# Six loads of a weight matrix begun from ScalarE's DMA queue instead of SyncE's

## The chip, the cores and the metric

The kernel runs on one core of a Trainium2 chip. A core has five engines with an instruction stream each: TensorE (PE in the profile; its weight loads are PEld), VectorE (DVE), ScalarE (ACT), GpSimd (POOL) and SyncE (SP). SyncE does no arithmetic here, it only begins DMA transfers. Sixteen DMA engines move the data. SPq and ACTq are the queues of the DMAs that SyncE and ScalarE begin. The metric is the time of one execution on the device in microseconds (us), shorter is better.

## The reference

Attention with a threshold on the scores (4 batches, 8 heads, 576 positions, width 64), and behind it two gated layers on 2304 tokens of width 512 with an inner width of 2048. All inputs and outputs are fp32.

```python
scores = scale * np.matmul(q, k.transpose(0, 1, 3, 2))
thresh = np.max(scores, axis=-1, keepdims=True) - tau
scores = np.where(scores >= thresh, scores, -1000000000.0)
scores = scores - np.max(scores, axis=-1, keepdims=True)
attn = np.exp(scores)
attn = attn / (np.sum(attn, axis=-1, keepdims=True) + 1e-09)
x = np.matmul(attn, v)                    # heads put side by side: 2304 x 512
...
h = x @ w_in                              # moe: w_in is 512 x 2048
g = h * np.tanh(sp)                       # sp = log1p(exp(h))
x = g @ w_out
...
h = x @ w_in                              # moe2
g = h * np.clip(h + 3.0, 0.0, 6.0) / 6.0
return (g @ w_out).astype(np.float32)
```

## The kernel before

Every instruction belongs to a named step, and the order of all steps is written out by hand in one long string, `SEQUENCE` (line 65), whose words are `step@engine`. Each engine works through its own steps in the order of that string, and a step waits on semaphores for the steps that it needs. So a step that is late holds up everything behind it on its engine.

Steps that matter here, with `n` for a pair of heads, `c` for a tile of 128 queries and `j` for one of the two heads:

- `lk`, `lq`, `lv`: loads of keys (line 1641), queries (1644) and values (1619), begun by SP.
- `s` (1707): scores on PE. `pk` (1716): their row maximum on DVE. `ex` (1726): the exponential on ACT. `th` (1721): the threshold on ACT. `mk` (1729): the mask on DVE, which also frees the score bank. `ph` (1734): rounding to fp16 on ACT. `pl` (629): the fp16 remainder on POOL.
- `tr` (1742): a transpose of the rounded tile by DMA, begun by SP, behind `pl`. `pv` (1755): the product with the values on PE, which needs the transposed tile.
- `dt`, `dr`, `dn`, `fl`, `xh`, `xl`: scaling the result, turning it on PE and splitting it into two fp16 parts, which are the input x of the first layer.

The first input weight, `moe_w_in`, comes as raw 64-bit words in eight groups of 1 MB. For a group `g`, `lr0_g` (line 764) begins the load, `zw0_g` (686, DVE) takes the column maxima, `zd`, `zp`, `zt`, `zf` make a scale of them (ACT, PE, DVE), `c0_g_` (805, ACT) scales and rounds the words, `c0_g_0` and `c0_g_1` (812, POOL) and `c0_g_l` (825, DVE) finish the conversion, and `h0_g_` (845, ACT) and `u0_g_j` (629, POOL) split it into two fp16 parts. Groups 2 and 5 go to a buffer of their own (`rawe`), the others share two (`raw`); a buffer is free again after `c0_g_l`. The products of the first layer, `g..` (1117, PE), start when the first weights and the first 256 rows of x are there, and run between the attention steps until the attention is done. `t` (1165) takes their results out on ACT and `hs` (1173) stores them. The other weights follow later in the same way, with `lr1`, `lr2` and `lr3`.

All eight `lr0` loads are begun by SP, so in its stream they stand between transposes and other loads. `load_words` makes these steps:

Of the kernel before, what the change touches and what calls it, by code (L numbers as in the profile page):

```python
# [77 lines left out]
vm2_1@dve lr0_2@sp ex2_1_0@act fl0_0@pe pk2_1_1@dve pv1_0_0@pe vm1_1@dve xh0_0@act th2_1_0@act c0_1_0@pool tr2_0_0@sp  # L78
# [7 lines left out]
ph0_2_0@act dt2_0@dve s0_3_0@pe zw0_3@dve c0_2_1@pool ph0_2_1@act s1_2_0@pe dr2_0@dve pl0_2_0@pool lr0_4@sp dn2_0@dve
pk0_3_0@dve fl2_0@pe pv3_0_0@pe pk0_3_1@dve ex0_3_0@act xh2_0@act th0_3_0@act xl2_0@dve ex0_3_1@act pv3_1_0@pe
c0_2_0@pool mk0_3_0@dve tr0_2_0@sp mk0_3_1@dve ph0_3_0@act s0_4_0@pe c0_2_l@dve ph0_3_1@act s1_2_1@pe zd0_3@act
pl0_3_0@pool zp0_3@pe dt3_0@dve pk0_4_0@dve zt0_3@dve th0_4_0@act lk0_4@sp dr3_0@dve zf0_3@dve ex0_4_0@act lq0_4@sp
pk1_2_0@dve h0_2_@act mk0_4_0@dve tr0_3_0@sp zx0_0_1@act u0_2_0@pool dn3_0@dve ph0_4_0@act pk1_2_1@dve fl3_0@pe  # L90
ex1_2_0@act pv0_2_0@pe zw0_4@dve th1_2_0@act ex1_2_1@act mk1_2_0@dve xh3_0@act c0_3_@act vm3_1@dve s1_3_0@pe lr0_5@sp
zd0_4@act mk1_2_1@dve s1_3_1@pe c0_3_1@pool ph1_2_0@act ph1_2_1@act s1_4_0@pe pk1_3_0@dve pl0_4_0@pool pk1_3_1@dve
ex1_3_0@act xl3_0@dve th1_3_0@act ex1_3_1@act u0_2_1@pool tr0_4_0@sp mk1_3_0@dve zp0_4@pe zt0_4@dve g00_0_0_0@pe
zf0_4@dve c0_3_0@pool g00_2_0_0@pe g00_4_0_0@pe lk0_5@sp g00_6_0_0@pe c0_4_@act lq0_5@sp g00_8_0_0@pe g00_10_0_0@pe
qp4@pool c0_3_l@dve g01_0_0_0@pe g01_2_0_0@pe pv0_3_0@pe c0_4_0@pool h0_3_@act lr0_6@sp g01_4_0_0@pe dt0_2@dve
# [10 lines left out]
ex2_3_0@act pl2_2_0@pool g31_4_0_0@pe g31_6_0_0@pe zf0_5@dve ex2_3_1@act g31_8_0_0@pe hs1_0_0@sp g31_10_0_0@pe
g40_0_0_0@pe th2_3_0@act xs0_4@sp g40_2_0_0@pe vh4@act g40_4_0_0@pe mk2_3_0@dve pv1_3_0@pe zx0_0_2@act mk2_3_1@dve
ph2_3_0@act u0_4_1@pool tr2_2_0@sp g40_6_0_0@pe g40_8_0_0@pe c0_5_@act dt1_2@dve dr1_2@dve zw0_6@dve s2_4_0@pe
s3_2_0@pe t3_0_0@act dn1_2@dve c0_5_0@pool pk2_4_0@dve ph2_3_1@act g40_10_0_0@pe g41_0_0_0@pe lr0_7@sp g41_2_0_0@pe
c0_5_1@pool pk3_2_0@dve g41_4_0_0@pe th2_4_0@act lk0_6@sp g41_6_0_0@pe ex2_4_0@act fl1_2@pe lq0_6@sp pv1_4_0@pe  # L110
# [474 lines left out]
def fused_kernel(ctx: ExitStack, tc, q, k, v, tau, w1i, w1o, w2i, w2o, out):  # L585
    nc = tc.nc
# [3 lines left out]
    add = plan.add  # L590
# [1447 lines left out]
```

## Time and profile before

| | |
|---|---|
| median of 3 runs | 966.33 us (966.15 to 967.31) |
| the profiled execution | 967.36 us, of which 965.5 us are the span from the first to the last instruction |
| PE busy | 920.3 us, 95% of the span |
| DVE, ACT, POOL busy | 767.3, 647.9, 402.5 us |
| DMA issues by SP | 217 plain ones and 80 transposes |

The profile comes from a single execution. Its views give, among others, the busy time of each engine by stretches of the span; a timeline of instructions by engine, with the idle time before each and what ended it in square brackets; the chain of work that ended last; and for DMA issues the time to landing. A row of a timeline has the start, the duration, engine, line, operation, output and inputs, and how many instructions are merged in it. For SPq and ACTq the duration is that of the issue on the queue, not that of the transfer. PEclk is the share of its full clock that TensorE was granted.

### The profile page before, as it was taken

What the parts mean: (1) busy time and instruction counts of PE and PEld (TensorE: products, weight loads), DVE (VectorE), ACT (ScalarE), POOL (GpSimd) and SP (SyncE); (2) the same over time, 40 slices, a digit from 0 to 9 for tenths busy, and PEclk for the clock granted to TensorE, in tenths of its full rate; (3) what the DMA queues carried; (4) which work ended last, traced back from release to release, by engine and by line L of the source; (5) the groups of instructions that cost most, each with busy time, mean ns of one, the idle gap of its engine ahead of it and who ended that gap; (6) DMA issues with size and microseconds to landing.
All of it is one profiled execution on the core that took longest, in us unless ns stands there. A gap on an engine that the chain in (4) does not pass through costs nothing.

```text
span 965.5 us, 25780 instructions
## 1 busy us (share of the span) xinstructions
PE 920.3 (95%) x10776; PEld 796.3 (82%) x10776; DVE 767.3 (79%) x1432; ACT 647.9 (67%) x1051; POOL 402.5 (42%) x354
## 2 busy tenths in 40 slices
PE   4679799999999999999999999999999999999998
PEld 2457577777777788888888888999999999999997
DVE  7997888778879887469999879787758858847865
ACT  6779877888789876568866878565444545536541
POOL 2778775756655766125656777710000000000000
PEclk9979999999999999999999999999999999999999
DMA  9999999999999999764665757760110101201001
GB/s 311 225 246 233 262 242 232 256 206 232 224 255 270 210 224 224 253 242 161 235 228 195 273 180 269 248 231 2 61 47 17 61 25 39 62 23 40 24 1 45
DMA packets 201796, 164.46 MB, mean 170 GB/s; under 512 B 174160, under 2 KB 174928, under 8 KB 195280
## 3 DMA queue, kind: packets, MB, share of 16 engines
q1 hardware_dynamic: 201296, 162.62, 62.5%
q8 instruction: 85, 1.39, 0.6%
q10 hardware_dynamic: 384, 0.20, 0.1%
q14 instruction: 31, 0.25, 0.1%
HBM read 84.28 MB, written 36.04 MB: 125 GB/s over the span
## 4 chain that ended last, share of the span: by engine, by line
PE 75%; DVE 15%; DMA 5%; ACT 1%; issue 1%; POOL 1%; SPq 1%; DVEq 0%; ACTq 0%; POOLq 0%
PE h_g L1117 14%; PE y_y L1231 13%; PE s_s L1707 7%; PE hp_g1a L1304 5%; PE h_g0a L1304 5%; PE aux_pv L1755 5%; DMA pt_tr<-p_ph 4%; PE hp_g1d L1304 2%; PE h_g0d L1304 2%; DVE e_ex L1729 2%; DVE nm_pk L1716 2%; DVE top L686 1%; PE h_g1b L1304 1%; PE hp_g0b L1304 1%; DVE gs_gh L1211 1%
## 5 line engine op out<-in xcount | busy, mean ns | idle before, releaser
L629 POOL TENSOR_TENSOR p_ph<-e_ex,p_ph 128x128 f16<-128x128 f32 (+3 forms) x160 | 186.9, 1190 | 119.1 <-ACT p_ph L1734 62.7
L1454 PEld LDWEIGHTS <-gs_oh 128*128 128x128 f16 x1512 | 146.9, 98 | 16.5
L1304 PEld LDWEIGHTS <-w__h 128*128 128x128 f16 x2016 | 156.0, 98 | 0.6
L1729 DVE SCALAR_TENSOR_TENSOR e_ex<-s_s,thr_th,e_ex 128x576 f32<-128x576 f32 x136 | 106.2, 812 | 19.8 <-ACT thr_th L1721 14.3
L1716 DVE TENSOR_REDUCE nm_pk<-s_s 128x1 f32<-128x576 f32 x136 | 98.6, 751 | 23.3 <-PE s_s L1707 22.0
L1726 ACT ACTIVATE e_ex<-s_s,nm_pk 128x576 f32<-128x576 f32 x136 | 98.3, 729 | 20.0 <-DVE nm_pk L1716 18.5
L1734 ACT ACTIVATE p_ph<-e_ex 128x576 f16<-128x576 f32 x144 | 94.8, 679 | 8.7 <-DVE e_ex L1729 6.7
L1304 PEld LDWEIGHTS <-w__u 128*128 128x128 f16 x1008 | 98.6, 98 | 0.0
L1755 PEld LDWEIGHTS <-pt_tr 128*128 128x128 f16 x2016 | 79.3, 101 | 19.2 <-DMA pt_tr<-p_ph 11.2
L1755 PE MATMUL aux_pv<-vh,pt_tr 128*128 128x65 f16 (+1 forms) x1296 | 85.2, 202 | 6.8 <-DMA pt_tr<-p_ph 6.7
L629 DVE TENSOR_TENSOR gs_oh<-g_ab,gs_oh 128x896 f16<-128x896 f32 x72 | 74.6, 1085 | 15.2 <-ACT gs_oh L1404 15.2
L1707 PE MATMUL s_s<-kd_lk,qs_qp 64*128 64x288 f32 x416 | 71.1, 455 | 7.4 <-DVE e_ex L1729 6.3
L1404 ACT ACTIVATE gs_oh<-g_ab 128x1792 f16<-128x1792 f32 x36 | 59.6, 1690 | 27.5 <-DVE g_ab L629 24.4
L1755 PE MATMUL aux_pv<-vl_vl,pt_tr 128*128 128x64 f16 x720 | 69.6, 201 | 0.0
L1388 ACT ACTIVATE g_ab<-g_ab,aux,hscales 128x512 f32<-128x512 f32 x72 | 54.1, 805 | 17.1 <-DVE g_ab L1332 17.1
L1707 PEld LDWEIGHTS s_s<-kd_lk,qs_qp 64*128 64x128 f32 x416 | 37.5, 195 | 26.6 <-issue 15.1
L1202 ACT ACTIVATE hp_e<-hl_l 128x512 f32<-128x512 f32 x72 | 42.5, 596 | 21.2 <-DVE gs_gh L1211 20.7
L1165 ACT ACTIVATE he_t<-h_g,hin 128x512 f32<-128x512 f32 x63 | 42.9, 682 | 18.4 <-PE h_g L1117 14.2
L1394 DVE SCALAR_TENSOR_TENSOR g_ab<-g_ab,f 128x512 f32<-128x512 f32 x72 | 51.2, 745 | 5.0 <-ACT g_ab L1388 5.0
L1211 DVE SCALAR_TENSOR_TENSOR gs_gh<-hp_e,fscales,gs_gh 128x512 f16<-128x512 f32 x72 | 52.8, 741 | 1.7 <-ACT gs_gh L1205 1.7
L1205 ACT ACTIVATE gs_gh<-hp_e,fscales 128x512 f16<-128x512 f32 x72 | 47.4, 680 | 9.9 <-PE y_y L1231 9.3
L1322 ACT ACTIVATE s_ka<-h_g0a 128x512 f32<-128x512 f32 x27 | 16.1, 595 | 48.4 <-PE h_g0a L1304 48.2
(662 smaller groups left out, 2555.8 us busy)
## 6 DMA issues: line engine op xcount, KB each, us to landing
hd<-he_t SPq DMA_DIRECT2D x36, 512.0 KB, 4.2
hl_l<-hd SPq DMA_DIRECT2D x18, 1024.0 KB, 5.6
raw_lr<-in_moe_w_out SPq DMA_DIRECT2D x16, 1024.0 KB, 7.4
raw_lr<-in_moe_w_in SPq DMA_DIRECT2D x14, 1024.0 KB, 6.1
yd<-yl_zhy SPq DMA_DIRECT2D x9, 896.0 KB, 3.6
qs_qp<-in_q SPq DMA_DIRECT2D x11, 576.0 KB, 4.9
v_lv<-in_v SPq DMA_DIRECT2D x16, 320.0 KB, 4.3
kd_lk<-in_k SPq DMA_DIRECT2D x15, 288.0 KB, 4.9
```

Source lines behind the costliest of these rows:

```text
L629: engine[e].tensor_tensor(dst, a, b, ALU.subtract)
L1117: mm(hv[:, j, :], wj[:, wl, c * P : (c + 1) * P], x.tile[:, c, xl, :], start=j == 0 and n == 0, stop=j == 1 and n == 11, skip_group_check= ...
L1211: nc.vector.scalar_tensor_tensor(s.tile[:, k, 1], g.tile.rearrange("p (a n) -> p a n", a=2), fs[:, fp : fp + 1], s.tile[:, k, 0], ALU.mult ...
L1231: mm(yv[:, h, :], wt[1][f // 2].tile[:, f % 2, wl, c * P : (c + 1) * P], gs[fp // COL].tile[:, fp % COL, gl, f % 2, :], start=fp == 0 and ...
L1304: mm(dst.tile[:, i * Q : (i + 1) * Q], wt[2][fp][wl].tile[:, right - 1, c * P : (c + 1) * P], x[xl].tile[:, c, left - 1], start=first and ...
L1454: mm(region(p), part[:, gl, left - 1], wt[3][fp][wl].tile[:, right - 1], start=fp == n == 0 and spot(p)[1] == 0, stop=fp == NG - 1 and n == 2,
L1707: mm(s[j].tile[:, half, :HALF], lh[r], rh[r], start=m == 0, stop=m == len(terms) - 1,)
L1716: nc.vector.tensor_reduce(neg.tile[:, j : j + 1], sv(j), AX.XY, ALU.max, negate=True)
L1726: nc.scalar.activation(ev(j), sv(j), AF.Exp, bias=neg.tile[:, j : j + 1])
L1729: nc.vector.scalar_tensor_tensor(ev(j), sv(j), thr.tile[:, j : j + 1], ev(j), ALU.is_ge, ALU.mult)
L1734: nc.scalar.activation(p16.tile[:, j, :S], e_.tile[:, j], AF.Copy)
L1755: mm(ov[:, dst, :d], pt.tile[:, j, ch, :], part.tile[:, src, vc, :], start=i == j == ch == 0 and part is vh, stop=j == w - 1 and ch == 8, ...
```

## The change

Six of the eight loads of the first input weight, `lr0_2` to `lr0_7`, are begun by ACT. `lr0_0` and `lr0_1` stay with SP, as do the loads of the other three weights, all transposes and all loads of queries, keys and values. The words keep their places in `SEQUENCE` (the rest of the string's diff is re-wrapped lines), so on ACT each load now stands behind the last ACT step that is written ahead of it: `lr0_2` behind `c0_1_`, `lr0_3` behind `ph3_0_1`, `lr0_4` behind `ph0_2_1`, `lr0_5` behind `c0_3_`, `lr0_6` behind `h0_3_` and `lr0_7` behind `ph2_3_1`. The transfers themselves, their buffers and what waits for them are the same.

```diff
-vm2_1@dve lr0_2@sp ex2_1_0@act fl0_0@pe pk2_1_1@dve pv1_0_0@pe vm1_1@dve xh0_0@act th2_1_0@act c0_1_0@pool tr2_0_0@sp
+vm2_1@dve lr0_2@act ex2_1_0@act fl0_0@pe pk2_1_1@dve pv1_0_0@pe vm1_1@dve xh0_0@act th2_1_0@act c0_1_0@pool tr2_0_0@sp
...
+zw0_2@dve fl1_0@pe s3_1_1@pe pl3_0_0@pool lr0_3@act pk3_1_0@dve pv2_0_0@pe pk3_1_1@dve ex3_1_0@act s0_2_0@pe
...
+s0_3_1@pe ph0_2_0@act dt2_0@dve s0_3_0@pe zw0_3@dve c0_2_1@pool ph0_2_1@act s1_2_0@pe dr2_0@dve pl0_2_0@pool lr0_4@act
...
+lr0_5@act zd0_4@act mk1_2_1@dve s1_3_1@pe c0_3_1@pool ph1_2_0@act ph1_2_1@act s1_4_0@pe pk1_3_0@dve pl0_4_0@pool
...
+g00_10_0_0@pe qp4@pool c0_3_l@dve g01_0_0_0@pe g01_2_0_0@pe pv0_3_0@pe c0_4_0@pool h0_3_@act lr0_6@act g01_4_0_0@pe
...
+s2_4_0@pe s3_2_0@pe t3_0_0@act dn1_2@dve c0_5_0@pool pk2_4_0@dve ph2_3_1@act g40_10_0_0@pe g41_0_0_0@pe lr0_7@act
...
     def load_words(raw, src, tag):
         def go(e):
-            nc.sync.dma_start(out=raw.tile, in_=src)
-
-        return add(("sp",), go, [], [raw], tag)
+            queue = nc.scalar if e == "act" else nc.sync
+            queue.dma_start(out=raw.tile, in_=src)
+
+        return add(("sp", "act"), go, [], [raw], tag)
```

## Rows read from the trace of the kernel before

**Rows 1.** The page: busy tenths and clock in 40 slices.
```profile
PE   4679799999999999999999999999999999999998
DVE  7997888778879887469999879787758858847865
```

**Rows 2.** Windows: start and end, length, busy of PE, PEld, DVE, ACT, POOL, PEclk.
```profile
30.00:66.00 36.00, 24.01 (x287) 17.27 (x286) 34.48 (x67) 27.06 (x50) 27.84 (x25) 0.85 1.07 237
66.00:140.00 74.00, 65.98 (x707) 49.24 (x708) 61.82 (x126) 62.46 (x115) 58.48 (x57) 0.91 1.09 248
```

**Rows 3.** Timeline of SP's queue from 34 us.
```profile
34.10 0.59 SPq L1644 DMA_DIRECT2D qs_qp<-in_q  x1
34.74 0.59 SPq L764 DMA_DIRECT2D rawe_lr<-in_moe_w_in  x1
35.51 6.87 SPq L1742 DMA_TRANSPOSE pt_tr<-p_ph  x1
```

**Rows 4.** The same queue from 90 us.
```profile
90.21 3.48 SPq L1742 DMA_TRANSPOSE pt_tr<-p_ph  x1
...
95.10 0.95 SPq L1644 DMA_DIRECT2D qs_lq<-in_q  x1
96.56 6.08 SPq L1742 DMA_TRANSPOSE pt_tr<-p_ph  x1
```

**Rows 5.** DMA issues begun near 34.8, 94.2, 95.1 and 51.5 us; us to landing last.
```profile
rawe_lr<-in_moe_w_in SPq DMA_DIRECT2D x1, 1024.0 KB, 7.5
raw_lr<-in_moe_w_in SPq DMA_DIRECT2D x1, 1024.0 KB, 5.1
qs_lq<-in_q SPq DMA_DIRECT2D x1, 576.0 KB, 7.5
v_lv<-in_v SPq DMA_DIRECT2D x1, 320.0 KB, 3.3
```

**Rows 6.** The chain that ended last: start, us, what.
```profile
34.10 4.41 DMA qs_qp<-in_q
...
96.56 9.04 DMA pt_tr<-p_ph
```

**Rows 7.** Timeline of PE, two of its waits.
```profile
38.56 0.76 PE L1707 MATMUL s_s<-kd_lk,qs_qp 64*128 64x288 f32 x4 [0.70 <-DMA qs_qp<-in_q]
...
105.65 0.20 PE L1755 MATMUL aux_pv<-vh,pt_tr 128*128 128x65 f16 x1 [1.25 <-DMA pt_tr<-p_ph]
```

**Rows 8.** Timeline of DVE around 40 us and at 74 us.
```profile
39.36 0.76 DVE L1716 TENSOR_REDUCE nm_pk<-s_s 128x1 f32<-128x576 f32 x1
40.33 0.76 DVE L1716 TENSOR_REDUCE nm_pk<-s_s 128x1 f32<-128x576 f32 x1 [0.21 <-PE s_s L1707]
...
74.42 0.16 DVE L1792 TENSOR_SCALAR den_dt<-aux_pv 128x4 f32<-128x4 f32 x1 [1.37 <-PE aux_pv L1755]
```

**Rows 9.** Timeline of ACT: what follows the places of three moved loads.
```profile
33.87 0.73 ACT L1726 ACTIVATE e_ex<-s_s,nm_pk 128x576 f32<-128x576 f32 x1
...
37.46 0.68 ACT L1734 ACTIVATE p_ph<-e_ex 128x576 f16<-128x576 f32 x1 [1.25 <-DVE e_ex L1729]
...
45.21 0.74 ACT L1726 ACTIVATE e_ex<-early_s,nm_pk 128x576 f32<-128x576 f32 x1 [1.50 <-DVE nm_pk L1716]
...
93.27 0.29 ACT L1721 ACTIVATE thr_th<-nm_pk,ntau 128x1 f32<-128x1 f32 x1 [0.18 <-DVE nm_pk L1716]
```

**Rows 10.** The two stretches in which ACT begins DMAs: first and last microseconds.
```profile
0.74 0.41 ACTq L600 DMA_DIRECT2D tau_sb<-in_tau  x1
...
961.11 1.86 ACTq L1511 DMA_DIRECT2D out<-s_vg  x3
```

**Rows 11.** Windows as in rows 2, around a fall of the clock.
```profile
96.00:100.00 4.00, 1.39 (x9) 0.64 (x8) 3.93 (x9) 3.12 (x5) 2.67 (x4) 0.96 0.98 339
100.00:104.00 4.00, 4.00 (x44) 2.78 (x41) 2.68 (x7) 3.84 (x8) 3.64 (x5) 0.61 1.16 256
```

More of the change, by code (lines that the diff above doesn't have):

```diff
@@ L86 @@
[L86 to L95, printed above, removed]
@@ L106 @@
[L106 to L110, printed above, removed]
@@ new lines @@
+ex1_4_0@act g10_6_0_0@pe g10_8_0_0@pe pv0_4_0@pe u0_3_0@pool kh0_4@act tr1_2_0@sp mk1_4_0@dve ex2_2_0@act
+g10_10_0_0@pe dt0_4@dve s2_2_1@pe zw0_5@dve u0_3_1@pool ph1_3_1@act xh0_2@act g11_0_0_0@pe ph1_4_0@act g11_2_0_0@pe
+dr0_4@dve c0_4_1@pool xl0_2@dve g11_4_0_0@pe g11_6_0_0@pe pk2_2_1@dve dn0_4@act g11_8_0_0@pe g11_10_0_0@pe ph1_3_0@act
+g20_0_0_0@pe c0_4_l@dve fl0_4@pe g20_2_0_0@pe th2_2_0@act g20_4_0_0@pe t1_0_0@act pl1_3_0@pool g20_6_0_0@pe
+g20_8_0_0@pe mk2_2_0@dve g20_10_0_0@pe ex2_2_1@act g21_0_0_0@pe g21_2_0_0@pe g21_4_0_0@pe xh0_4@act kh0_5@act
@@ new lines @@
+tr3_2_0@sp g51_0_0_0@pe pk4_0_0@dve g51_2_0_0@pe th3_4_0@act g51_4_0_0@pe ex3_4_0@act g51_6_0_0@pe qp7@pool
+u0_6_1@pool dn2_2@dve g51_8_0_0@pe ph3_3_1@act g51_10_0_0@pe zp0_7@pe g60_0_0_0@pe zt0_7@dve fl2_2@pe mk3_4_0@dve
+g60_2_0_0@pe pl3_3_0@pool xh2_2@act g60_4_0_0@pe pv2_4_0@pe t5_0_0@act xl2_2@dve zf0_7@dve ph3_4_0@act lk0_7@sp
+s4_0_1@pe dt2_4@dve c0_7_@act pk4_0_1@dve g60_6_0_0@pe g60_8_0_0@pe pl3_4_0@pool tr3_3_0@sp g60_10_0_0@pe ex4_0_0@act
+dr2_4@dve dn2_4@dve g61_0_0_0@pe g61_2_0_0@pe g61_4_0_0@pe th4_0_0@act g61_6_0_0@pe ex4_0_1@act mk4_0_0@dve
@@ new lines @@
+ph5_1_0@act s6_0_1@pe lv1_2@sp vl6@dve ph5_1_1@act pv4_1_0@pe vh7@act pk6_0_0@dve pl5_1_0@pool g00_6_0_1@pe
+ex6_0_0@act dt4_0@dve g00_8_0_1@pe pk6_0_1@dve g00_10_0_1@pe g01_0_0_1@pe g01_2_0_1@pe dr4_0@dve th6_0_0@act
+g01_4_0_1@pe ex6_0_1@act g01_6_0_1@pe mk6_0_0@dve g01_8_0_1@pe g01_10_0_1@pe tr5_1_0@sp g10_0_0_1@pe mk6_0_1@dve
+t0_0_1@act g10_2_0_1@pe g10_4_0_1@pe g10_6_0_1@pe ph6_0_0@act dn4_0@dve g10_8_0_1@pe g10_10_0_1@pe vm0_2@dve
+g11_0_0_1@pe ph6_0_1@act g11_2_0_1@pe s6_1_0@pe pl6_0_0@pool s6_1_1@pe lv2_2@sp pk6_1_0@dve hs7_0_0@sp fl4_0@pe
@@ new lines @@
+pk6_1_1@dve pv5_0_0@pe ex6_1_0@act zf1_1@dve th6_1_0@act g11_4_0_1@pe ex6_1_1@act g11_6_0_1@pe mk6_1_0@dve
+g11_8_0_1@pe tr6_0_0@sp g11_10_0_1@pe xh4_0@act g20_0_0_1@pe mk6_1_1@dve ph6_1_0@act g20_2_0_1@pe g20_4_0_1@pe
+g20_6_0_1@pe xl4_0@dve ph6_1_1@act s7_0_0@pe vl7@dve s7_0_1@pe t1_0_1@act pl6_1_0@pool pk7_0_0@dve c1_1_@act
+hs1_0_1@sp pv5_1_0@pe pk7_0_1@dve g20_8_0_1@pe ex7_0_0@act dt5_0@dve g20_10_0_1@pe dr5_0@dve vm2_2@dve g21_0_0_1@pe
+g21_2_0_1@pe th7_0_0@act g21_4_0_1@pe ex7_0_1@act mk7_0_0@dve g21_6_0_1@pe c1_1_0@pool g21_8_0_1@pe tr6_1_0@sp
@@ new lines @@
+hs3_0_1@sp th4_2_0@act ex4_2_1@act g40_4_0_1@pe mk4_2_0@dve g40_6_0_1@pe g40_8_0_1@pe g40_10_0_1@pe mk4_2_1@dve
+ph4_2_0@act g41_0_0_1@pe tr7_1_0@sp g41_2_0_1@pe s4_3_0@pe vm3_2@dve ph4_2_1@act s4_3_1@pe dt6_0@dve ve2@dve
+pl4_2_0@pool dr6_0@dve pk4_3_0@dve zdv2_2@act g41_4_0_1@pe g41_6_0_1@pe g41_8_0_1@pe dn6_0@dve g41_10_0_1@pe
+ex4_3_0@act g50_0_0_1@pe pk4_3_1@dve fl6_0@pe pv7_0_0@pe xh6_0@act th4_3_0@act xl6_0@dve ex4_3_1@act g50_2_0_1@pe
+tr4_2_0@sp mk4_3_0@dve g50_4_0_1@pe t4_0_1@act g50_6_0_1@pe g50_8_0_1@pe mk4_3_1@dve g50_10_0_1@pe ph4_3_0@act
@@ new lines @@
+g51_0_0_1@pe s4_4_0@pe ph4_3_1@act s5_2_0@pe pl4_3_0@pool pk4_4_0@dve lk0_8@sp pv7_1_0@pe lq0_8@sp pk5_2_0@dve
+th4_4_0@act ex4_4_0@act g51_2_0_1@pe dt7_0@dve g51_4_0_1@pe dr7_0@dve g51_6_0_1@pe ex5_2_0@act mk4_4_0@dve
+g51_8_0_1@pe g51_10_0_1@pe g60_0_0_1@pe qp8@pool tr4_3_0@sp t5_0_1@act g60_2_0_1@pe dn7_0@dve g60_4_0_1@pe c1_0_l@dve
+g60_6_0_1@pe ph4_4_0@act g60_8_0_1@pe s5_2_1@pe pl4_4_0@pool pk5_2_1@dve fl7_0@pe pv4_2_0@pe xh7_0@act kh0_8@act
+xl7_0@dve tr4_4_0@sp g60_10_0_1@pe g61_0_0_1@pe th5_2_0@act g61_2_0_1@pe ex5_2_1@act mk5_2_0@dve g61_4_0_1@pe
@@ new lines @@
+g61_6_0_1@pe h1_0_@act g61_8_0_1@pe hs5_0_1@sp g61_10_0_1@pe mk5_2_1@dve g70_0_0_1@pe lr1_2@sp s5_3_0@pe ph5_2_0@act
+xs3_4@sp s5_3_1@pe u1_0_0@pool t6_0_1@act pk5_3_0@dve g70_2_0_1@pe ph5_2_1@act pk5_3_1@dve g70_4_0_1@pe pv4_3_0@pe
+ex5_3_0@act pl5_2_0@pool g70_6_0_1@pe th5_3_0@act ex5_3_1@act dt4_2@dve g70_8_0_1@pe dr4_2@dve mk5_3_0@dve
+g70_10_0_1@pe g71_0_0_1@pe g71_2_0_1@pe mk5_3_1@dve g71_4_0_1@pe ph5_3_0@act g71_6_0_1@pe g71_8_0_1@pe g71_10_0_1@pe
+dn4_2@dve ph5_3_1@act s5_4_0@pe tr5_2_0@sp c1_1_l@dve t7_0_1@act s6_2_0@pe pl5_3_0@pool pk5_4_0@dve fl4_2@pe
```

141 lines of the change are left out of this document (58 added, 83 removed).

## The prediction

> **What bounds the kernel now.** I read the page first. In the 40 slices, of 24 us each, PE is at 9 tenths from the sixth slice on, and the early slices are those in which PE has 4 to 7 tenths and DVE up to 9 [rows 1]. So behind some 140 us the time is PE's work, and what this change can win or lose lies ahead of that, where the six loads are begun (34 to 94 us). The windows cut that stretch in two [rows 2]. From 30 to 66 us DVE is busy for 34.48 of 36 us: DVE is the bound, and the most that could be won there, if it never waited, is 36 - 34.48 = 1.5 us. From 66 to 140 us PE has 65.98 of 74 us, and its waits are what can be won.
>
> I then asked whether the loads themselves are late for anyone, in the list of waits from 26 to 100 us: no wait of DVE or ACT for a raw weight word stands in it. So an earlier load is worth nothing by itself. What is left is what the loads do to their neighbours: to SP's stream, to the transfers beside them, and now to ACT's stream.
>
> **SP's side: what is removed.** The load of 34.74 costs SP 0.59 us of issue [rows 3]; six of them are at most 3.5 us. SP is free of it at 35.33 and begins the next transpose at 35.51; behind each of the six there is such a gap, mostly because the transpose waits for POOL's remainder. So the issue time itself gives nothing: POOL sets the pace, and if it didn't, the 3.5 us would be spread over SP's stream, for which DVE doesn't wait.
>
> The transposes behind the loads do gain. The one at 35.51 lasts 6.87 us, to 42.38, and the load of 34.74 lands 7.5 us after its issue, at 42.2 [rows 3, 5]. The one at 96.56 lasts 6.08 us, to 102.64, with the queries of 95.10 landing at 102.6 [rows 4, 5]. Nothing of that kind ahead, a transpose takes 3.48 us (90.21). I read from this that a transpose is held on SP's queue until the plain load ahead of it in the same queue has landed. With the load on ACT's queue this hold goes or shrinks: up to 6.87 - 3.48 = 3.4 us at 35.51, and at 96.56, where 1 MB leaves the queue ahead of keys and queries, up to 6.08 - 3.48 = 2.6 us.
>
> Who waits for these transposes? Ahead of 66 us nobody on the chain, DVE being the bound. At 105.65 PE does: 1.25 us idle for the transpose of 96.56, which took 9.04 us and is on the chain [rows 6, 7]. The landing 1.25 us sooner is well within the 2.6 us, so this wait goes. What comes behind it is not all free, since the next scores need a bank that DVE's mask frees a moment later; bounds 0 and 1.25 us, and I take 1.0 us as the gain, nearer to the full row because other banks are free.
>
> **ACT's side: what is added.** ACT gets six issues. The trace has ACT beginning DMAs only in its first and last microseconds: 0.41 us for one, 1.86 us for three, so 0.41 to 0.62 us each [rows 10], at most 6 x 0.62 = 3.7 us together. Where ACT has slack they are hidden. Behind `ph3_0_1` ACT idles for 1.50 us until 45.21 [rows 9]; `lr0_3` falls there, and `lr0_4` and `lr0_6` fall in two more idle stretches of this sort. `lr0_2` pushes the exponential of 33.87 back by some 0.5 us, and ACT idles for 1.25 us at 37.46 for DVE. `lr0_5` delays `zd0_4` and what follows, near 67 us, and DVE has 1.37 us of waiting at 74.42 [rows 8] that takes it up. `lr0_7` stands in front of the threshold of 93.27, where ACT waited only 0.18 us, and the exponential behind it leads over DVE to PE's scores: 0.41 - 0.18 = 0.2 us lost. No buffer makes ACT wait: that of `lr0_2` is new, and for the other five ACT has, earlier in its own order, done the `h0` step of the group that had the buffer (`h0_3_` stands right ahead of `lr0_6`), and this step waits for the same conversion that frees it.
>
> Whether ACT is held when SP's queue is in the middle of a transpose isn't to be seen, as ACT begins nothing beside one. Bounds: nothing, or until that transpose's issue is over. For `lr0_7`, reached at 93.07, that is until 93.69 and then 0.41 to 0.62 us, so up to 1.0 us instead of 0.2. I take 0.2, the row of a plain issue under traffic, 0.59 us at 34.74, being nearer to it than a hold.
>
> **The transfers: what collides.** Ahead of `lr0_2` SP begins the queries of pair 3 at 34.10; they land 4.41 us later and PE, which has waited for 0.70 us, starts their scores at 38.56 [rows 3, 6, 7]. DVE takes the maxima at 39.36 without any idle time ahead and waits 0.21 us for the second at 40.33 [rows 8]. So these queries are on the path of the engine that is the bound, without slack. In one queue the weight words, begun at 34.74, come behind them. ACT reaches `lr0_2` at about 33.87 [rows 9], so now the 1 MB starts in another queue at about the same moment as the 576 KB. The lower bound of the delay is 0, if SP's queue goes first. The upper bound is the whole of the 1 MB: 1024 KB landed in 5.1 us at best and 320 KB in 3.3 us [rows 5], so 704 KB more cost 1.8 us, and 1024 KB, by estimate from these rows, 2.6 us. With equal shares, 576 KB of the weight words go beside the queries: 576 / 1024 x 2.6 = 1.5 us. I take that. It is paid in full: DVE's order is fixed and it has next to no idle time up to 66 us, and PE's start of the first layer follows it.
>
> The Trainium skill has two rules here, on the page "DMA: Bandwidth & Descriptors". Its section "Queues, rings and completion order" says that SP and ACT each own a row of rings on the same 16 DMA engines, which serve the rows in turn packet by packet, and share the descriptor generator. It speaks for the delay of the queries and for ACT being held; no row of this trace shows two queues at work together, so it can't be tested here. The section "Issuing engines are not separate DMA queues" says that beginning DMAs on several engines saves only the issue time of the sequencer. By that rule the hold behind the loads would not go away and the sum would be that of the third rival below.
>
> **The sum.** On the profiled execution, 967.36 us (965.5 of span and 1.9 around it): +1.5 for the queries, +0.2 for ACT at 93.27, -1.0 for the wait at 105.65, so +0.7 us. The profiled execution is 1.0 us above the median of the runs, 966.33; on the median the sum gives 967.0 us.
>
> **The rivals.** *Slower.* The loads on ACT's queue are served ahead of what SP has begun. Then the whole 1 MB goes ahead of the queries of 34.10 (+2.6 us), and at 94 us `lr0_7`, begun at 93.1 by ACT, still goes ahead of the keys and the queries of 95.10, so that the transpose of 96.56 is held as now and nothing is won at 105.65: 2.6 + 0.2 = +2.8 us, 969.1 us. It decides from the point where two thirds of the 1 MB, (1.9 - 0.2) / 2.6, go ahead of the queries. For it: the load is begun first or together, and the queries have no slack. Against it: nothing in the trace gives ACT's queue the right of way.
>
> *Faster.* The queries land as now, the freed transposes win 1.25 us at 105.65 and 0.2 us of DVE's wait at 40.33, and with the shorter gaps TensorE keeps its clock. Its falls are dear: in the stretch from 96 to 100 us PE is busy for 1.39 of 4 us, and from 100 to 104 us the granted clock is 0.61, so mostly the lower level of 1.2 GHz [rows 11], which costs PE 39% of 4 us, 1.6 us. From 66 to 140 us the clock is 0.91 in the mean [rows 2], so there are more of these. With one fall less the sum is -1.25 - 0.2 - 1.6 = -3.0 us, 963.3 us; if the fall goes in part, 964.0 us. It decides only if a fall goes, since the first two terms are within 1.9 us. Against it: only one of the freed transposes has PE waiting for it. A fall more, as likely with PE's start put off, would go to the slower case.
>
> *Nothing changes.* The hold of the transposes comes from the traffic, not the queue; the loads arrive as before, and ACT's six issues fall into its slack: 966.3 us, within 0.2 us of it.
>
> **How the numbers follow.** No change is what lies within 0.2%, 1.9 us, about what a measurement of this kernel can tell. The sum of +0.7 us has 0.42, of which 0.08 is past +1.9 us; slower has 0.20; faster has 0.24, of which 0.03 stays within 1.9 us; nothing has 0.14. So faster 0.21, same 0.34 + 0.03 + 0.14 = 0.51, slower 0.28. The range leaves out about a tenth on each side: on top that half of the slower case in which a fall of the clock comes on the 2.8 us, so it ends at 970.0; below that part of the faster case in which a whole fall goes, so it begins at 963.8. The likeliest case's own range is 965.5 to 968.9: the delay of the queries at 0 (-1.5 us) or 2.6 us (+1.1), and ACT held on top of that (+0.8).
>
> **What would show it.** The queries at 34.10 should land 5 to 7 us after their issue and DVE should wait over a microsecond at 40.33; if they land in 4.4 us, that step is wrong. The transposes behind the old places of the loads should last 3.3 to 4.5 us on SP's queue; if they still take 5 to 7 us, the reading of the hold is wrong. PE's wait at 105.65 should be gone. ACT's six issues should take 0.4 to 0.6 us; several microseconds would mean that ACT is held. What would make the whole wrong is a fall of the clock that comes or goes, or a load on ACT that waits for something I have not seen and holds up the exponentials.

## The result, and the profile after

The changed kernel takes 978.64 us in the median (976.60 to 980.47, 4 runs), the kernel before 966.82 us beside it (966.15 to 969.41): the ratio is 1.0117, 95% interval 1.0086 to 1.0147. That is slower by 11.8 us, where 967.0 us and no change were forecast, and outside the range of 963.8 to 970.0. The profiled execution has a span of 975.6 us, 10.1 us more than before.

The page of the changed kernel, busy tenths as in [rows 1]:

```profile
PE   4659789999999999999999999999999999999998
DVE  7778689878788888469999889878848847857865
```

And the windows of [rows 2] (the last two numbers are the busy share of the DMA engines and the GB/s that they moved):

```profile
30.00:66.00 36.00, 22.28 (x246) 15.64 (x247) 28.76 (x54) 22.15 (x38) 25.95 (x24) 0.94 0.93 218
66.00:140.00 74.00, 60.49 (x588) 43.72 (x586) 56.75 (x119) 58.11 (x106) 51.55 (x53) 0.85 0.98 223
```

The loss is where it was looked for, ahead of 140 us, but the reader should look at DVE: it is busy for 28.76 of 36 us instead of 34.48, so it is no longer the bound up to 66 us; it waits. PE has 5.5 us less work in the second stretch.

DVE has the same instructions in the same order in both kernels, so its lateness can be read off instruction by instruction. This is the start of some of them against the kernel before, in us, for the two profiled executions (worked out from the timelines):

```
start in the kernel before   36.61  41.45  59.45  61.32  74.42  105.95  110.78  130.02  247.53  960.61
later in the changed one     -0.51   3.37   3.19   7.70   7.08    7.09   11.39   12.31    9.81   10.16
```

The loss comes in three steps: 3.9 us at about 40 us, 4.5 us at 60 us, 4.3 us at 107 us; some 2 us are given back behind 130 us. Each has one of the moved loads beside it. The timeline of the two queues (those of [rows 3] and [rows 4], with ACT's issues of `lr0_2`, `lr0_4` and `lr0_7`):

```profile
30.30 3.39 SPq L1743 DMA_TRANSPOSE pt_tr<-p_ph  x1
...
31.98 0.34 ACTq L765 DMA_DIRECT2D rawe_lr<-in_moe_w_in  x1
...
33.74 0.59 SPq L1645 DMA_DIRECT2D qs_qp<-in_q  x1
34.84 5.55 SPq L1743 DMA_TRANSPOSE pt_tr<-p_ph  x1
...
57.40 0.33 ACTq L765 DMA_DIRECT2D raw_lr<-in_moe_w_in  x1
...
97.29 3.70 SPq L1743 DMA_TRANSPOSE pt_tr<-p_ph  x1
...
97.91 0.34 ACTq L765 DMA_DIRECT2D raw_lr<-in_moe_w_in  x1
...
103.82 8.68 SPq L1743 DMA_TRANSPOSE pt_tr<-p_ph  x1
```

On SP's queue the load stood behind the transpose's issue, 3.4 to 4.0 us after its start. ACT begins it 1.7, 1.2 and 0.6 us after the start (the transpose beside `lr0_4` began at 56.16), while the transpose is still being issued. The DMA issues, with us to landing last, first `lr0_2` and the transpose of 30.30, then the queries of 33.74, then `lr0_4` and the transpose of 56.16, then `lr0_7` and the transpose of 97.29:

```profile
rawe_lr<-in_moe_w_in ACTq DMA_DIRECT2D x1, 1024.0 KB, 6.4
pt_tr<-p_ph SPq DMA_TRANSPOSE x1, 8.2
...
qs_qp<-in_q SPq DMA_DIRECT2D x1, 576.0 KB, 6.6
...
raw_lr<-in_moe_w_in ACTq DMA_DIRECT2D x1, 1024.0 KB, 6.7
pt_tr<-p_ph SPq DMA_TRANSPOSE x1, 7.8
...
raw_lr<-in_moe_w_in ACTq DMA_DIRECT2D x1, 1024.0 KB, 10.6
pt_tr<-p_ph SPq DMA_TRANSPOSE x1, 12.3
```

In the kernel before, the first two of these transposes, of 30.81 and 52.80:

```profile
pt_tr<-p_ph SPq DMA_TRANSPOSE x1, 5.3
...
pt_tr<-p_ph SPq DMA_TRANSPOSE x1, 5.1
```

The third, of 90.21, landed after 5.2 us, the queries after 4.41 us [rows 6] and the load of 94.22 after 5.1 us [rows 5]. So the transposes that were already under way are late by 2.9, 2.7 and 7.1 us, and in the last pair the load is late as well.

In the first two pairs it is only the end of the transpose that is late. A transpose moves 2304 packets of 256 bytes; 32 packets of 4 bytes go with it, and it lands 0.5 to 0.6 us behind the last of these. The packet records of the transpose of 30.30 show the 256-byte packets done at 35.26 (35.62 before), but the 4-byte packets run from 37.39 to 37.83, where they ran from 35.43 to 35.63 before: behind the 128 packets of the load, which run from 35.06 to 37.81. Between 35.4 and 37.0 us 91 packets move, all of them the load's. Beside `lr0_4` it is the same: 256-byte packets done at 60.80, 4-byte packets at 63.38, the load's last at 63.37.

Who pays is in the timeline of PE. Two waits of the kernel before are in [rows 7], 0.70 us for the queries and 1.25 us for the transpose of 96.56; a third was for the transpose of 52.80, here with the scores behind it:

```profile
57.94 0.20 PE L1755 MATMUL aux_pv<-vh,pt_tr 128*128 128x65 f16 x1 [0.67 <-DMA pt_tr<-p_ph]
...
58.96 1.24 PE L1707 MATMUL s_s<-kd_lk,qs_lq 64*128 64x288 f32 x8
```

In the changed kernel:

```profile
38.49 0.23 PE L1756 MATMUL aux_pv<-vh,pt_tr 128*128 128x65 f16 x1 [2.87 <-DMA pt_tr<-p_ph]
...
40.40 1.33 PE L1708 MATMUL s_s<-kd_lk,qs_qp 64*128 64x288 f32 x4 [0.20 <-DMA qs_qp<-in_q]
...
64.06 0.24 PE L1756 MATMUL aux_pv<-vh,pt_tr 128*128 128x65 f16 x1 [3.60 <-DMA pt_tr<-p_ph]
...
65.70 2.29 PE L1708 MATMUL s_s<-kd_lk,qs_lq 64*128 64x288 f32 x8
...
115.43 0.20 PE L1756 MATMUL aux_pv<-vh,pt_tr 128*128 128x65 f16 x1 [4.14 <-DMA pt_tr<-p_ph]
```

and behind PE in that of DVE (39.36 and 40.33 of [rows 8] are here 41.78 and 43.70):

```profile
41.78 0.76 DVE L1717 TENSOR_REDUCE nm_pk<-s_s 128x1 f32<-128x576 f32 x1 [1.38 <-PE s_s L1708]
43.70 0.76 DVE L1717 TENSOR_REDUCE nm_pk<-s_s 128x1 f32<-128x576 f32 x1 [1.16 <-PE s_s L1708]
...
68.04 0.76 DVE L1717 TENSOR_REDUCE nm_pk<-s_s 128x1 f32<-128x576 f32 x1 [2.07 <-PE s_s L1708]
...
118.73 0.76 DVE L1717 TENSOR_REDUCE nm_pk<-s_s 128x1 f32<-128x576 f32 x1 [1.86 <-PE s_s L1708]
```

The waits are not the whole loss: behind each of them PE works at about half its speed for some microseconds. The eight scores of 65.70 take 2.29 us where they took 1.24; the granted clock is 0.50 from 64 to 68 us, the lower level of 1.2 GHz, and was 1.00 from 58.0 to 60.5 in the kernel before. Behind the tile of 115.43 it is 0.57 from 116 to 120 us (1.00 from 106.0 to 108.5 before). At the first step the granted clock reads 1.00, but the scores of 40.40 and the two groups behind them take 1.33, 1.17 and 1.17 us, as they do in `e6_later` at a granted clock of 0.50, and 0.76, 0.65 and 0.65 in the kernel before. PE, too, has the same instructions in the same order in both kernels, and comparing them one by one puts sizes on this (lateness of PE in us, worked out from the timelines):

```
              ahead of the tile   at the tile   behind the scores
first step          -0.5              2.3              3.4
second step          3.2              6.1              7.8
third step           7.0              9.8             11.3
```

At the first step the wait of 0.70 us for the queries has shrunk to 0.20, so that PE is 1.8 us late when the scores begin. So the late tiles cost 2.3, 2.9 and 2.8 us and the slow work 1.5, 1.7 and 1.5 us.

The chain that ended last shows the same transfers: where [rows 6] has queries of 4.41 us and one transpose of 9.04 us, it now has

```profile
33.74 6.62 DMA qs_qp<-in_q
...
56.16 7.85 DMA pt_tr<-p_ph
...
103.82 11.56 DMA pt_tr<-p_ph
```

In the first step it runs over the queries, since they landed 0.16 us behind the moment at which PE was through with the late tile. The transpose of 103.82 is that of [rows 4] at 96.56. Its own load is gone from in front of it, but the transfers ahead of it, and with them its issue (8.68 us instead of 6.08), are late because of the collision at 97.

### The profile page after: what moved, and what is told of

The parts are those of the page before. It is cut to its first block, busy times and chain, and to the rows that moved or that the text cites. A ratio compares the mean times of both kernels' runs of the same rounds, so it can differ in the third digit from the quotient of the medians.

```text
span 975.6 us, 25780 instructions
## 1 busy us (share of the span) xinstructions
PE 925.1 (95%) x10776; PEld 799.2 (82%) x10776; DVE 767.5 (79%) x1432; ACT 648.6 (66%) x1051; POOL 402.5 (41%) x354
## 4 chain that ended last, share of the span: by engine, by line
PE 84%; DVE 9%; DMA 4%; issue 1%; ACT 1%; POOL 0%; SPq 0%; DVEq 0%; ACTq 0%
PE h_g L1118 17%; PE y_y L1232 17%; PE s_s L1708 9%; PE aux_pv L1756 6%; PE h_g0a L1305 5%; PE hp_g1a L1305 5%; DMA pt_tr<-p_ph 3%; PE hp_g1d L1305 2%; PE h_g0d L1305 2%; DVE e_ex L1730 2%; DVE nm_pk L1717 2%; PE h_g1b L1305 1%; PE hp_g0b L1305 1%; PE y_y___1_7_0_14515 L1455 1%; PE y_y___1_6_0_13903 L1455 1%; PE y_y___1_5_0_13243 L1455 1%
## 5 line engine op out<-in xcount | busy, mean ns | idle before, releaser
L1756 PE MATMUL aux_pv<-vh,pt_tr 128*128 128x65 f16 (+1 forms) x1296 | 85.8, 203 | 12.9 <-DMA pt_tr<-p_ph 12.9
L1708 PE MATMUL s_s<-kd_lk,qs_qp 64*128 64x288 f32 x416 | 74.5, 474 | 6.7 <-DVE e_ex L1730 6.3
```

Source lines behind the costliest of these rows:

```text
L1708: mm(s[j].tile[:, half, :HALF], lh[r], rh[r], start=m == 0, stop=m == len(terms) - 1,)
L1756: mm(ov[:, dst, :d], pt.tile[:, j, ch, :], part.tile[:, src, vc, :], start=i == j == ch == 0 and part is vh, stop=j == w - 1 and ch == 8, ...
```

## The experiments

The theory after the result, called collision: a large load begun in a second queue while a transpose of SP's queue is under way makes the transpose, and at times the load too, land late, and the time is lost where PE waits for that transpose at once. The rivals: a cost spread over all six loads (bandwidth, or ACT's issue time), the queries of pair 3 alone (the prediction's own step), and a cost of ACT's queue wherever the load stands. The lateness of DVE in each profile, at the same instructions as above, and the timed ratio to the kernel before:

```
                             36.61  41.45  61.32  74.42  105.95  110.78  130.02  247.53  960.61   ratio, 95% interval
changed kernel               -0.51   3.37   7.70   7.08    7.09   11.39   12.31    9.81   10.16   1.0117 (1.0086 to 1.0147)
e1_lr2                       -0.59   3.36   3.19   2.57    2.59    2.11    2.10    0.41    3.66   1.0012 (0.9999 to 1.0025)
e2_lr457                     -0.23  -0.10   4.81   5.61    5.63    6.84    5.71    3.53    3.94   1.0091 (1.0059 to 1.0123)
e3_lr36                       0.14   0.23   0.71   0.32    0.35   -0.16   -0.16   -3.35   -1.44   1.0000 (0.9983 to 1.0016)
e11_lr7                       0.17   0.24   0.05  -0.09   -0.08    3.70    4.69    2.18    2.36   1.0019 (0.9999 to 1.0040)
e12_quarter                  -0.02   0.03   0.03  -0.13   -0.12   -0.16   -0.09   -1.39   -1.46   1.0014 (0.9997 to 1.0031)
e6_later                     -0.62   1.25   1.06   0.45    0.44    0.10    0.19   -2.86   -2.91   1.0002 (0.9978 to 1.0026)
e9_later_sp2                  0.25   0.42   0.22   0.02    0.02   -0.66   -0.67   -2.47   -1.58   0.9996 (0.9974 to 1.0019)
e5_tiny_dram                  0.17   1.40   1.66   1.07    1.06    1.31    0.07   -1.12   -1.18   0.9999 (0.9981 to 1.0016)
e4_tiny                       0.28   2.17   1.98   1.95    1.98    2.55    2.31    7.71   10.70   1.0084 (1.0062 to 1.0106)
e10_tile                     -0.31   0.01  -0.18  -1.13   -1.12   -1.28   -0.70    0.06    2.75   1.0049 (1.0027 to 1.0071)
```

Up to 130 us the columns are mostly clean steps. Behind 130 us most kernels drift by 1 to 3 us against this one profile of the kernel before, with or without a moved load; the changes are judged by the steps.

**One part at a time.** Three kernels leave some of the six words with SP.

```diff
-lr0_2@sp
+lr0_2@act
```

> Only lr0_2 is begun by ACT, the other five by SP. Theory, collision: a 1 MB load in ACT's queue that starts while a transpose of SP's queue is under way makes both land late, and whoever needs the transpose pays. lr0_2 started beside the transpose of 30.30, which took 8.15 us instead of 5.29; the stretch up to the exponential of before's 45.21 lost 3.3 us. So 969 to 971 us, and the lost time within 30 to 46 us. Rival, spread cost (bandwidth shared, or ACT's issue time): a sixth of the 11.8 us lost in all, 968 to 969 us. Rival, the queries of pair 3 alone (the prediction's step): +1.5 us, with the loss seen at DVE's wait for these scores and the transposes on time.

968.99 us, and the whole loss of 3.9 us sits at 40 us, as in the changed kernel. Some of it is given back by 75 us, and the timed ratio says only 1.2 thousandths, an interval that still holds 1. What PE waited for ahead of the scores of pair 3:

```profile
38.53 0.24 PE L1756 MATMUL aux_pv<-vh,pt_tr 128*128 128x65 f16 x1 [2.99 <-DMA pt_tr<-p_ph]
...
40.38 1.33 PE L1708 MATMUL s_s<-kd_lk,qs_qp 64*128 64x288 f32 x4
```

It waited 2.99 us for the tile of the transpose beside the load, which landed after 8.3 us, and then only 0.14 us, too short for the view to name what ended it: the queries, landed 6.7 us after their issue, were there for scores that were late already. So the rival of the queries alone, which wanted the transposes on time, falls.

```diff
-lr0_4@sp ... lr0_5@sp ... lr0_7@sp
+lr0_4@act ... lr0_5@act ... lr0_7@act
```

> Only lr0_4, lr0_5 and lr0_7 are begun by ACT: the three that started 1.2, 3.4 and 0.6 us behind the start of a transpose that was still under way. Collision: most of what is lost behind 46 us comes back, +6 to +9 us, 973 to 976 us, with each of the three landing 6.5 us or more after its issue and the transpose beside it 8 us or more. Spread cost: half of the loss, +6 us, so about 972.7 us, and then the kernel with lr0_3 and lr0_6 must cost a third, +4 us.

976.07 us: the larger part. `lr0_4`, begun at 54.12, landed after 6.6 us and the transpose of 52.92 beside it after 8.0 us; DVE lost 4.9 us. `lr0_5` and `lr0_7` took 9.3 and 9.9 us and the transposes beside them 12.9 and 10.7 us, but cost DVE only 0.8 and 1.2 us here. Behind the wait at the third step, 3.01 us at 112.49, the granted clock stayed at 1.00 (112.5 to 116.5 us), so the slow work that followed it in the changed kernel is missing. The profile is that of the fastest of the five runs, 971.20 us; it shows less of the loss than the median has.

```diff
-lr0_3@sp ... lr0_6@sp
+lr0_3@act ... lr0_6@act
```

> Only lr0_3 and lr0_6 are begun by ACT: the two that started with no transpose under way (the next one was begun 3.3 and 3.8 us later). Collision: nothing lost, 966 to 968 us. Spread cost (bandwidth, or ACT's issue time, or that the loads leave SP's order): a third of the loss, +4 us, 970.5 us.

966.27 us, nothing lost: the spread cost, which wanted +4 us, falls. But one premise of mine was wrong as well. In this kernel `lr0_3` did start beside a transpose, 0.6 us behind it (42.70 and 43.27); the DMA issues of the two, with us to landing last:

```profile
raw_lr<-in_moe_w_in ACTq DMA_DIRECT2D x1, 1024.0 KB, 6.5
pt_tr<-p_ph SPq DMA_TRANSPOSE x1, 9.7
```

So the collision was there, 9.7 us instead of 6.4. PE waited 1.07 us for that tile at 52.41, but DVE was at most 0.7 us late behind it and on time again by 111 us. The theory has to be in two parts: the collision makes the transpose late, and the place decides who pays.

**One load alone, and a quarter of it.**

```diff
-lr0_7@sp
+lr0_7@act
```

> Only lr0_7 is begun by ACT, at its place in the change, 0.6 us behind the start of a transpose. Theory, collision: the transpose of about 90.2 lands 9 us or more after its begin instead of 5.16, lr0_7 likewise instead of 5.1, and DVE is 3 to 4.5 us late from 108 us on, as it was in the change: 969 to 971 us. Rival, the loss at 108 us came from the lateness brought along from 40 and 60 us: no loss here, 966.8 us, or the gain of 1 us that the prediction gave to the freed transpose behind it.

969.61 us, with 3.8 us lost from 106 to 111 us and none before (the interval of the timed ratio just holds 1). From 74 to 106 us DVE is within 0.1 us of the kernel before, so the same 10 us can be laid side by side. The DMA view of `e11_lr7` from 90 to 100 us, in 40 slices (the tenths are the busy share of the 16 DMA engines; q1 is SP's queue, q10 ACT's; then packets, MB, share), and of the DMA issues begun from 90 to 91 us:

```profile
DMA  9630069996993100192299196099929999999929
GB/s 442 145 79 0 0 128 213 158 40 148 666 36 34 33 0 0 34 201 34 34 237 101 34 237 101 34 372 507 473 105 429 425 291 281 56 118 108 70 8 30
DMA packets 1869, 1.61 MB, mean 161 GB/s; under 512 B 1711, under 2 KB 1711, under 8 KB 1740
...
q10 hardware_dynamic: 144, 1.05, 54.0%
...
raw_lr<-in_moe_w_in ACTq DMA_DIRECT2D x1, 1024.0 KB, 9.5
pt_tr<-p_ph SPq DMA_TRANSPOSE x1, 11.9
```

The same view of the kernel before; then a line of its window from 96 to 98 us, in which only packets of loads move, and the transpose among the issues from 90 to 91 us:

```profile
DMA  9732029993008999999299514898979978989998
GB/s 426 260 77 73 0 53 218 201 44 8 0 5 183 291 287 292 292 290 190 39 131 262 98 33 197 360 524 360 492 262 360 459 295 318 329 313 341 313 258 249
DMA packets 2888, 2.30 MB, mean 230 GB/s; under 512 B 2528, under 2 KB 2528, under 8 KB 2758
...
q1 hardware_dynamic: 92, 0.75, 97.8%
...
pt_tr<-p_ph SPq DMA_TRANSPOSE x1, 5.2
```

Before, from 93 us on (the 13th slice), the transpose moves at 290 GB/s and is done. With the load beside it, the GB/s go to 34 and to 0, with short bursts up to 237, for some 3.5 us, and in the 10 us 1.61 MB move instead of 2.30. So in this pair the two do not only share the rate, the rate falls. A packet of the load takes 10 us x 16 x 0.540 / 144 = 0.60 us in the mean, against 2 us x 16 x 0.978 / 92 = 0.34 us in the kernel before; the 144 include 16 packets of 4 bytes, and the 128 others alone take 0.67 us. That is not so in every pair: the load's packets took 0.32 us beside the transpose of 30.30 and 0.34 us beside that of 56.16, and in the 10 us from the start of the former 2.51 MB moved, against 2.14 MB in the kernel before.

```diff
-g41_0_0_0@pe lr0_7@sp g41_2_0_0@pe
+g41_0_0_0@pe lx0_7@act lr0_7@sp g41_2_0_0@pe
...
-            nc.sync.dma_start(out=raw.tile, in_=src)
+            ps = slice(32, P) if tag == "lr0_7" else slice(0, P)
+            nc.sync.dma_start(out=raw.tile[ps], in_=src[ps])
...
+                add(("act",), lambda e, raw=raw, g=g: nc.scalar.dma_start(
+                    out=raw.tile[:32], in_=src[g][:32]), [], [raw], "lx0_7")
```

> lr0_7 is cut in two: 32 of its 128 rows (256 KB) are begun by ACT at the place of lr0_7 in the change, 0.6 us behind the start of a transpose; the other 96 rows stay on SP's queue at the old place. If the transpose is delayed in proportion to what the second queue moves: of the 6.8 us that the whole MB added in e11_lr7 (11.92 us instead of 5.16), a quarter, so a landing after some 7 us, and no loss at 108 us beyond 1 us. If a second queue of 8 KB packets stops the transpose for a fixed time: 9 us or more again and 2 to 3.4 us lost at 108 us.

967.75 us, and DVE is on time at 111 us. The two issues of 90 to 91 us:

```profile
raw_lx<-in_moe_w_in ACTq DMA_DIRECT2D x1, 256.0 KB, 5.5
pt_tr<-p_ph SPq DMA_TRANSPOSE x1, 7.4
```

The transpose is late by 2.3 us for a quarter and by 6.8 us for the whole. A quarter of 6.8 is 1.7, so the delay grows with what the load moves; a fixed part of about a microsecond is not excluded, as the small transfers below show.

**The same queue, later.** The edit in short, with the step behind which each load stands:

```diff
-lr0_2@act (behind c0_1_)   ... lr0_3@act (ph3_0_1) ... lr0_4@act (ph0_2_1) ... lr0_5@act (c0_3_)  ... lr0_7@act (ph2_3_1)
+lr0_2@act (behind th2_1_0) ... lr0_3@act (ex3_1_0) ... lr0_4@act (ex0_3_0) ... lr0_5@act (ex1_3_0) ... lr0_7@act (ex3_2_0)
```

> All six loads are begun by ACT, but five of them some 1 to 3 us later, behind an ACT step that waits for DVE at about the time when SP began them in the kernel before: lr0_2 behind th2_1_0, lr0_3 behind ex3_1_0, lr0_4 behind ex0_3_0, lr0_5 behind ex1_3_0, lr0_7 behind ex3_2_0. Each should then start when the issue of the transpose ahead of it is over. Theory, collision: what costs is a load begun in a second queue while SP's transpose is still being read, so most of the 11.8 us comes back: 966 to 970 us, with the transposes ahead of the loads landing in 4 to 6 us. Rival, ACT's queue or ACT's issues cost wherever they stand: 975 us or more.

966.48 us: with all six loads still on ACT's queue the 11.8 us are gone. `lr0_4` now starts at 57.68, 0.2 us behind the end of the issue of the transpose of 54.04, and the DMA issues of the two are

```profile
raw_lr<-in_moe_w_in ACTq DMA_DIRECT2D x1, 1024.0 KB, 6.1
...
pt_tr<-p_ph SPq DMA_TRANSPOSE x1, 5.1
```

with 5.1 us where the changed kernel has 7.8. A cost of ACT's queue or of its issues wherever they stand falls. This is the experiment that settles the cause of the second and third step: only the start of the loads against the transposes was changed.

```diff
-lr0_2@act
+lr0_2@sp
```

> As e6_later, with lr0_2 back on SP's queue at its old place, so that the queries of pair 3 stay ahead of it. Collision: the five others still start behind the transposes' issue and cost nothing; e6_later lost 1.9 us at 40 us and this should come back, 963.5 to 966 us, the fastest yet if so. Rival, what e6_later lost there was TensorE's clock (0.50 from 32 to 40 us in its profile) and not the load: 966.5 us again.

967.38 us beside 968.58 of the kernel before, ratio 0.9996: the 1.9 us at 40 us came back in the profile (0.2 instead of 1.9), the timed ratio is that of `e6_later`. In `e6_later` the granted clock was 0.50 from 32 to 40 us, the lower level of 1.2 GHz, and the queries landed 4.6 us after their issue instead of 4.4; so it speaks for the rival that the clock, not the load, cost them. Neither kernel beats the one before.

**Without transposes.** Both kernels with plain copies of the same bytes:

```diff
-nc.sync.dma_start_transpose(
+nc.sync.dma_start(
```

> The kernel before with each of the 80 transposes replaced by a plain copy of the same bytes, so the products behind it take tiles that are not transposed; everything else is the same, all loads with SP. It is the base for e8_plain_act: faster than the kernel before by what the transposes hold up, 955 to 966 us.

> The changed kernel with plain copies in place of the transposes as in e7_plain_sp (the tiles are not transposed). Theory, collision with transposes: the six loads on ACT now cost nothing to speak of, within 2 us of e7_plain_sp. Rival, bandwidth shared between two queues, whatever they carry: 5 us or more above e7_plain_sp. Rival, ACT's issue time: 10 us above it.

960.69 and 964.00 us (ratios to the kernel before 0.9930, 0.9905 to 0.9955, and 0.9968, 0.9953 to 0.9984): 3.3 us apart, between my two expectations. Nearly all of it comes in one place. DVE of `e8_plain_act` is 0.4 us early against that of `e7_plain_sp` at 37 us and 2.8 us late at 41.5 us; at 61 us it is 2.7 and at 111 us 3.2 us late, so the steps at 60 and 107 us are not there. The queries of pair 3, begun at 31.39 in the first kernel and at 30.98 in the second, each on a line of the DMA issues:

```profile
qs_qp<-in_q SPq DMA_DIRECT2D x1, 576.0 KB, 5.0
```

and in `e8_plain_act`, with what PE waited for them:

```profile
qs_qp<-in_q SPq DMA_DIRECT2D x1, 576.0 KB, 9.0
```

```profile
40.02 0.83 PE L1708 MATMUL s_s<-kd_lk,qs_qp 64*128 64x288 f32 x4 [2.72 <-DMA qs_qp<-in_q]
```

So `lr0_2` costs the queries even without a transpose, and it went ahead of them: the queries, begun 1.2 us before the load, moved their packets from 36.1 us on, the load from 33.1 to 37.4. The two larger steps are absent though the loads begin 1.2 and 0.6 us behind the start of the copies, as in the changed kernel: the copies landed within 0.4 us of those of `e7_plain_sp`. What a plain copy suffers that is further from its end is not shown, since these two had all but ended when the load's first packets moved (58.25 against 58.03 us, 96.17 against 95.89).

**Small transfers.** 4 bytes to each of 128 partitions, begun by ACT at the six places, once into a new tile in SBUF, once into DRAM, and the new tile alone (the edit in short):

```diff
+    tiny = const.tile([P, 8], F32, name="tiny")      # e4_tiny, e10_tile; in e5_tiny_dram: dram.tile
...
+    nc.scalar.dma_start(out=tiny[:, g : g + 1], in_=tau.partition_broadcast(P))      # not in e10_tile
```

> All loads with SP as before, and at the six places ACT begins an added transfer of 4 bytes to each of 128 partitions, which nobody reads: ACT's issue time and the use of a second queue, without the 1 MB. Collision of the 1 MB: 966 to 968 us, six issues of 0.3 to 0.6 us mostly hidden. Rival, ACT's issues hold up its exponentials: as slow as the change, 975 us or more. Rival, any use of a second queue beside a transpose upsets it, whatever its size: transposes of 8 us and more beside the tiny ones, and 970 us or more.

> The small transfers of e4_tiny again, to a scratch place in DRAM instead of a tile in SBUF, so that no tile of the kernel lies elsewhere than before. e4_tiny lost 2.5 us by 130 us and 8 us more between 130 and 330 us, where it begins nothing on ACT. If the shifted tiles did the latter: 967 to 970 us here, with the loss of some 2 us at 40 us that stays. If the small transfers did it: 974 to 976 us again. Collision of the 1 MB alone: 967 us and no loss at 40 us.

> The kernel before with the 32-byte tile of e4_tiny allocated and nothing else: no transfer on ACT. If the shifted tiles cost e4_tiny its time behind 130 us: 972 to 976 us. If the small transfers into SBUF did: 966.8 us.

975.01, 967.13 and 973.49 us. The first looked as if ACT's issues did the harm; the second, with the same issues, shows that they do not. The tile alone, 32 bytes in each partition that shift the tiles behind it, costs more than half of what `e4_tiny` lost, and all of it behind 130 us. Whether the rest is the writes into SBUF, and what in the shifted tiles costs, stays open. What the small transfers do beside a transpose is small: the transposes of 30.98 and 91.27 in `e5_tiny_dram` landed after 6.6 and 6.3 us instead of 5.3 and 5.2. The first of them cost DVE 1.2 us at 40 us, where the theory of the 1 MB alone had said none.

## Why the prediction was wrong

**The step that failed** is "The transfers: what collides". It looked for what is begun behind the load and gave a price to the queries of 34.10 alone; the transposes ahead of the load, still under way, got none. All three steps begin with PE waiting for such a tile, or at 107 us for that of the next transpose, which was late with them: 2.87 us where it had not waited, 3.60 for 0.67, 4.14 for 1.25. PE's lateness at these tiles is some 8 of the 12.7 us of the three steps, its slow work behind them most of the rest. With the loads some 1 to 3 us later (`e6_later`) the steps at 60 and 107 us are absent, as they are without transposes, and with `lr0_7` alone the one at 107 us stands alone. My slower rival was built on the queries as well, and so ended at 969.1 us.

**The queries** were late as foretold but were not what held PE. They landed 6.6 us after their issue, within the 5 to 7 us, so 2.2 us later than before: more than the 1.5 us taken, less than the bound of 2.6. DVE waited as foretold at 41.78 and 43.70, but PE waited only 0.20 us for them, and 0.14 us in `e1_lr2`, because the late tile stood ahead of them in its order. The two came late to the same moment, so what the queries alone would have cost here can't be read; without transposes it is 3.2 us, slow scores included. The load was ahead of the queries and not beside them: ACT's queue runs ahead of its compute steps and began `lr0_2` at 31.98, before the step written ahead of it, `c0_1_`, started at 32.26, and not at 33.87.

**"Ahead of 66 us nobody on the chain"** waits for the transposes: PE did wait, 0.67 us at 57.94, only DVE did not wait behind it. How much later a tile could be was not asked: 2.7 us more at 56.16 made PE wait 3.60 us.

**The transposes behind the loads** were to be freed: in small part right. That of 34.84 lasted 5.55 us on SP's queue instead of 6.87, not the 3.3 to 4.5 us foretold. That of 103.82 lasted 8.68 instead of 6.08. The hold itself was read rightly: these two end at 40.39 and 112.50, and the queries ahead of them in the same queue land at 40.36 and 112.81. The load left the queue, the queries stayed. So the gain of 1.0 us was not there to be had: the wait at 105.65 grew from 1.25 to 4.14 us, and in `e6_later`, without the collision, it is still 1.10 us.

**ACT's side** was right and too careful: the issues took 0.33 to 0.35 us, none was held, and the threshold of 93.27 [rows 9], here at 100.35, waited 0.18 us as before. The 0.2 us were not lost. The two kernels with small transfers in DRAM and with later loads confirm that the issues are free.

**The falls of the clock** stood in the rivals and in no term of the sum. The means of the two windows, 0.94 and 0.85 against 0.85 and 0.91 in [rows 2], hide what they did: some 1.5 us behind each of the three waits, about the 1.6 us that the faster rival had for one fall.

The Trainium skill says on the page "DMA: Bandwidth & Descriptors", section "Queues, rings and completion order", that the DMA engines serve the queues in turn, packet by packet. In part the traces agree: in `e3_lr36`, from 45.5 to 48 us, 88 packets of SP's queue move beside 90 of ACT's. The load's 128 packets are 8 for each of 16 engines, at 0.34 us an estimate of 2.7 us for a transpose that waits behind all of them. The first two pairs have that size, 2.9 and 2.7 us, but there the transpose's last packets came behind the whole load and not in turn with it. In `e11_lr7` the transpose was late by 6.8 us, with the rate down to 34 GB/s and less; at the 0.67 us that a packet took there, 8 packets are 5.4 us. By the section "Issuing engines are not separate DMA queues" only the sequencer's issue time would change; here the measurement decides against it, by 11.8 us. Why the 4-byte packets came last, and what slowed the packets in the last pair, could not be told from these traces.

## What to carry to other kernels

A single queue is also an order: here it kept a large load off a transpose that was still under way, and the load moved to a second queue lost this. Before moving a transfer, list what is in flight at the moment at which the new queue will begin it, which is earlier than the step in front of it in the code, and ask of each of these how much later it may land. If the load must be in the second queue, put it behind a step that waits until the transpose's issue is over. And count more than the wait: in the changed kernel PE worked at about half its speed for some microseconds behind each of the three waits, which added half as much again.

## What the runs showed of the hardware

- A load of 1 MB in a second queue, begun 0.6 to 1.7 us behind the start of a transpose of 576 KB, made it land 2.7 to 7.1 us later. In the worst pair alone (`e11_lr7`, 11.9 instead of 5.2 us) 1.61 MB moved in 10 us, where one queue moved 2.30 MB in the same 10 us with the load behind the transpose.
- In the two pairs of 2.9 and 2.7 us the transpose's 256-byte packets were done in time; its 32 packets of 4 bytes ran behind the load's last 8 KB packets, and it landed 0.6 us behind those.
- The delay grows with the load: at the place of `lr0_7` 6.8 us for 1 MB, 2.3 us for 256 KB and 1.2 us for 4 bytes to each of 128 partitions.
- A collision may cost next to nothing: 9.7 us for the transpose of 42.70 with `lr0_3` beside it, and DVE on time by 111 us.
- Behind waits of 3.60 and 4.14 us PE worked at a granted clock of 0.50 (64 to 68 us) and 0.57 (116 to 120 us); in `e2_lr457` it stayed at 1.00 behind a wait of 3.01 us.
- 32 bytes in each partition of SBUF that nothing uses, allocated ahead of most other tiles, made the kernel slower by a ratio of 1.0049 (1.0027 to 1.0071).
